# A two-operand form for three small VectorE instructions, and a later place for an output split and four matmuls, in an attention and expert kernel

## Chip, core and metric

The kernel runs on one core of one Trainium2 chip. The metric is the device time of one execution in microseconds. The core's engines run side by side, each through its own queue in order: TensorE (PE, with its weight loads PEld), VectorE (DVE), ScalarE (ACT), GpSimd (POOL) and SyncE (SP), which here only issues DMAs. GpSimd computes and also issues some DMAs.

## What is computed

Pooled attention (queries are averaged in pairs), then a dense block with the Mish activation, then eight experts whose outputs are weighted by a Sinkhorn-normalised gate. Only the first part is touched by the change:

```python
# q, k, v: (2, 8, 1152, 64)
q_pool = q.reshape(B, H, S // 2, 2, D).mean(axis=3)
scores = scale * np.matmul(q_pool, k.transpose(0, 1, 3, 2))
scores = scores - np.max(scores, axis=-1, keepdims=True)
attn = np.exp(scores)
attn = attn / (np.sum(attn, axis=-1, keepdims=True) + 1e-09)
attn_out = np.matmul(attn, v)
# then: h = x @ w_in; g = h * tanh(softplus(h)); g @ w_out; then the experts
```

## The kernel before

Products of fp32 accuracy are made of fp32r matmuls: an operand is split into a high part (a copy rounded to fp32r) and a low part (the operand less the high part). `split_hi` (L72) and `split_lo` (L80) issue these; on GpSimd they show as L78 and L81, on ScalarE as L74.

**Attention.** Sixteen heads go in eight pairs `p`; a pair has nine query tiles, so there are 72 steps `g = 9p + t`, and three more steps of tail. The order is written out by hand in the loop at L706 to L763. A step issues, in this order: `scores(g)` (six matmuls L469, twelve at t = 4, and on VectorE the copy out of PSUM with the row minimum, L474); the GpSimd preparation `prep(p, t)`; due VectorE work of the weights (`run(g, "dve")`); a first transposing job of the next tiles; `transposes(g - 3)` (nine PE transposes L551, ScalarE's high parts `eth` L554, VectorE's low parts `etl` L557); up to nine products of attention with values (`run_av`, PE L572); further transposing jobs (`trans_k`, `trans_q`, L401 and L447); and `exps(g)` (ScalarE L488). At its end it runs one entry of the list `late` and then all due weight work (`run_all`). The scores have one PSUM buffer, so `scores(g + 1)` waits for L474 of step g.

**GpSimd's work of a pair** (`PREP`, L626). For the next pair's queries `q0` to `q3` at t = 1 to 4 (L379, L78, L381, L81 on `qraw` and `qst`); for values and keys the high and low parts `v00`, `v01` at t = 1, 2, `k00`, `k01` at t = 2, 3, `v10` and `v11` both at t = 5, `k10` at t = 7, `k11` at t = 8 (L78 and L81 on `vst`, `kst`). After a low part GpSimd issues the DMA that refills the raw buffer (L338). GpSimd isn't held to the steps: it goes through its queue as far as data allow.

**Attention outputs.** The products of a pair come in four groups of 18, ready after t = 4, 7, 0 and 2 of the loop, and are run in the steps t = 5, 6; 8, 0; 1, 2; 3, 4. Step t = 7 has none. At the end of a group `evac` (L577) copies half of its bank on ScalarE (L581) and adds the halves on VectorE into the one buffer `xs` (L589). After the fourth group, at t = 4, it appends `split_x(p)` to `late` (L592), which that step's end runs: three GpSimd instructions, L598 (times the reciprocal row sums), L78 (`xh`) and L81 (`xl`). The next pair's first L589, at t = 6, writes the same buffer.

**Weights.** `w_in` and `w_out` arrive as 64-bit words and are brought to fp32 by `plan64` (L134 to L183): a scale (`scale(1)`, L147 on GpSimd or L149 on ScalarE), a second one on ScalarE (L151), `shift` (VectorE L156, a shift and a mask), `sign` (VectorE L162), `join` (GpSimd L168), then high and low part. Four pieces of the first `w_in` block (L616) go at t = 7 of pairs 1 to 4, with `busy=True` and in two halves: for one piece L156 comes at t = 0 and 2 and L162 at t = 1 and 3 of the next pair, `join` at t = 5, high part and low part (both GpSimd) at t = 6 and 7. Two pieces of `w_out` (L617) go at steps 52 (pair 5, t = 7) and 60 (pair 6, t = 6), also in halves, without `busy`. Later pieces (from L618) are not in halves.

`row_sums` (L496) adds epsilon to the nine row sums of a pair at t = 0 of the next (L498), VectorE's reciprocal L499 follows, and at t = 1 a PE transpose.

Of the kernel before, what the change touches and what calls it, by code (L numbers as in the profile page):

```python
# [8 lines left out]
F32 = mybir.dt.float32  # L9
# [3 lines left out]
U32 = mybir.dt.uint32  # L13
AF = mybir.ActivationFunctionType
ALU = mybir.AluOpType
# [8 lines left out]
def pool_attention_mish_sinkhorn_kernel(  # L24
# [12 lines left out]
    nc = tc.nc  # L37
    P = 128
# [8 lines left out]
    NPAIR = B * H // 2  # L47
    HPB = H // 2
    QTL = 2 * SQ // P
# [7 lines left out]
    EPS = 1e-9  # L57

    const = ctx.enter_context(tc.tile_pool(name="const", bufs=1))
# [6 lines left out]
    make_identity(nc, ident)  # L66
    identr = const.tile([P, P], F32R, name="identr")
    nc.vector.tensor_copy(identr, ident)
    ones = const.tile([P, P], F32, name="ones")
    nc.vector.memset(ones, 1.0)  # L70

# [44 lines left out]
    def load_w(which, i, times, stage, late="pool", parts=1, busy=False):  # L116

        src = w_sources(i)[which].rearrange("(c p) f -> p c f", p=P)
        nm = ("wu", "wd")[which]

        def dest():
            if i not in (w1t, w2t)[which]:
                pool = wpools[f"d{0 if i == NG1 else i % 2}" if which else i % 2]
                (w1t, w2t)[which][i] = tuple(
                    pool.tile([P, 4, GF], F32R, tag=nm + x, name=f"{nm}{x}{i}") for x in "hl")
            return (w1t, w2t)[which][i]

        def hi(heng, c, x):
            split_hi(heng, dest()[0][:, c, :], x)

        def lo(c, x):
            split_lo(nc.vector if late == "dve" else nc.gpsimd, dest()[1][:, c, :], x, dest()[0][:, c, :])

        def plan64(u, t):  # L134
            box = {}

            def dma():
                raw = wraw.tile([P, 2 * GF], F32, tag="raw", name=f"raw{which}_{i}_{u}")
                nc.sync.dma_start(out=raw.bitcast(I64), in_=src[:, u, :])
                w = raw.rearrange("p (n two) -> p n two", two=2)  # L140
                box["l"], box["h"] = w[:, :, 0], w[:, :, 1]

            def scale(x):
                if x and busy:
                    nc.gpsimd.tensor_scalar(box["h"], box["h"], 2.0 ** -112, 0.0, op0=ALU.mult, op1=ALU.add)  # L147
                elif x:
                    nc.scalar.activation(box["h"], box["h"], AF.Copy, scale=2.0 ** -112)  # L149
                else:  # L150
                    nc.scalar.activation(box["l"].bitcast(I32), box["l"].bitcast(U32), AF.Copy, scale=2.0 ** -29)  # L151

            def shift(cs=slice(0, GF)):
                if "t" not in box:
                    box["t"] = wpools["t"].tile([P, GF], U32, tag="wt", name=f"wt{which}_{i}_{u}")
                nc.vector.tensor_scalar(  # L156
                    box["t"][:, cs], box["h"][:, cs].bitcast(U32), 3, 0x7FFFFFF8,
                    op0=ALU.logical_shift_left, op1=ALU.bitwise_and)

            def sign(cs=slice(0, GF)):  # L160
                t = box["t"][:, cs]
                nc.vector.scalar_tensor_tensor(  # L162
                    out=t, in0=box["h"][:, cs].bitcast(U32), scalar=0x80000000, in1=t,
                    op0=ALU.bitwise_and, op1=ALU.bitwise_or)

            def join():
                t = box["t"].bitcast(I32)
                nc.gpsimd.tensor_tensor(out=t, in0=t, in1=box["l"].bitcast(I32), op=ALU.add)  # L168

            ts = t if isinstance(t, tuple) else [t + j * stage for j in range(5)]  # L170
            at(ts[0] - 2.4 * stage, "dma", dma)
            at(ts[0], "pool" if busy else "act", lambda: scale(1))
            at(ts[0] + parts - 1, "act", lambda: scale(0))
            for j in range(parts):
                cs = slice(j * GF // parts, (j + 1) * GF // parts)
                at(ts[1] + 2 * j, "dve", lambda cs=cs: shift(cs))
                at(ts[1] + 2 * j + parts - 1, "dve", lambda cs=cs: sign(cs))
            at(ts[2], "pool", join)
            if busy:
                at(ts[3], "pool", lambda: hi(nc.gpsimd, u, box["t"].bitcast(F32)))  # L180
            else:
                at(ts[3], "act", lambda: hi(nc.scalar, u, box["t"].bitcast(F32)))
            at(ts[4], late, lambda: lo(u, box["t"].bitcast(F32)))  # L183

        def plan32(u, t):
            box = {}

            def dma():
                raw = box["raw"] = wraw.tile([P, 2 * GF], F32, tag="raw", name=f"raw{which}_{i}_{u}")
                nc.sync.dma_start(out=raw.rearrange("p (c f) -> p c f", c=2), in_=src[:, 2 * u:2 * u + 2, :])  # L190

            def both(j):
                x = box["raw"][:, j * GF:(j + 1) * GF]
                hi(nc.gpsimd, 2 * u + j, x)
                lo(2 * u + j, x)

            at(t[0] - 2.4 * stage, "dma", dma)
            for j in range(2):
                if i == NG1:
                    at(t[j], "act", lambda j=j: hi(nc.scalar, 2 * u + j, box["raw"][:, j * GF:(j + 1) * GF]))  # L200
                    at(t[j] + 1, "pool", lambda j=j: lo(2 * u + j, box["raw"][:, j * GF:(j + 1) * GF]))
                else:
                    at(t[j], "pool", lambda j=j: both(j))

        if i < NG1:
            for u, t in enumerate(times):
                if t:
                    plan64(u, t)
        else:
            for u in range(2):  # L210
                plan32(u, times[2 * u:2 * u + 2])
        for q in queue.values():
            q.sort(key=lambda x: x[0])
# [77 lines left out]
    with ExitStack() as actx:  # L291
# [25 lines left out]
        tiny = pool("tiny", 4)  # L317
        wpools["t"] = pool("wt", 2)

        qz = []  # L320
        for i in range(2):
            t = z_p.tile([P, 2, 2, P], F32R, name=f"qz{i}")
# [172 lines left out]

        def row_sums(p):  # L496
            rs = rsS[p]
            nc.vector.tensor_scalar(rs, rs, EPS, None, op0=ALU.add)  # L498
            nc.vector.reciprocal(rs, rs)  # L499

        def turn_sums(p):
# [62 lines left out]
        def queue_av(p, gi):  # L564
# [12 lines left out]
            def evac():  # L577
                ps = box["ps"]
                b, hp, h0 = heads(p)
                t = o_p.tile([D, SQ - c0], F32, tag="t", name=f"avt{p}_{gi}")  # L580
                nc.scalar.activation(t[:, 0:n], ps[D:2 * D, 0:n], AF.Copy)  # L581
                s = s0 - j * (SQ + D)
                if p not in xs_t:
                    xs_t[p] = xs_p.tile([P, SQ], F32, tag="xs", name=f"xs{p}")
                xs = xs_t[p]
                a = max(0, -s)
                for s, a, b in ((SQ - D, 0, a), (s + a, a, n)):
                    if a < b:
                        nc.vector.tensor_tensor(  # L589
                            out=xs[j * D:(j + 1) * D, s:s + b - a], in0=ps[0:D, a:b], in1=t[:, a:b], op=ALU.add)  # L590
                if gi == len(GROUPS) - 1:
                    late.append(lambda: split_x(p))  # L592

            def split_x(p):
                b, hp, h0 = heads(p)
# [11 lines left out]
        def run_av(n):  # L607
            for _ in range(n):
                if av_todo:
                    av_todo.pop(0)()  # L610
# [3 lines left out]
        T0 = NQ + LAG + 1 - EARLY  # L614

        load_w(0, 0, [(t, t + 2, t + 7, t + 8, t + 9) for t in evenly(16, 9)], 2, parts=2, busy=True)  # L616
        load_w(1, 0, [(t, t + 2, t + 7, T0 + j, T0 + j + 1) for j, t in enumerate((52, 60))], 2, "dve", parts=2)  # L617
        load_w(1, 0, [None, None] + [(t, t + 1, t + 2, t + 3, t + 4) for t in (T0 + 1, T0 + 3)], 1, "dve")  # L618
        for m in range(1, 2 * NG1 - 1):
            load_w((m + 1) % 2, (m + 1) // 2, evenly(T0 + BPG * m - 3.5, 1.5), 1)  # L620
# [85 lines left out]
        for g in range(T0 + EARLY):  # L706
# [10 lines left out]
            if g < LAG:  # L717
                exps(g)
                for f in pre:
                    f()  # L720
                if g + 1 < LAG:
                    split_kv(0, 0, "v", nc.gpsimd, g)
                    scores(g + 2, ps_s)
            else:
                if LAG < g < NQ:
                    scores(g)
                if p and g < NQ:
                    prep(p, t)
                if g < T0:
                    run(g, "dve")  # L730
                if pre:
                    pre.pop(0)()
                ready = len(av_todo)
                if g < NQ + LAG:
                    transposes(g - LAG)
                if g <= NQ:
                    hand_over(g - 1)
                if not p:
                    prep(p, t)
                run_av(min(ready, 9 if g < NQ else 18))  # L740
                for f in pre:
                    f()
                if g < NQ:
                    exps(g)
# [578 lines left out]
```

## Time and profile before

| | us |
|---|---|
| median of three runs | 1241.89 |
| lowest, highest | 1239.9, 1243.31 |
| profiled execution | 1242.97 |
| its span, first to last instruction | 1240.5 |

| engine | busy us | share of the span |
|---|---|---|
| PE | 1212.8 | 98% |
| PEld | 1117.6 | 90% |
| DVE | 875.2 | 71% |
| ACT | 593.2 | 48% |
| POOL | 651.4 | 53% |

The profiled execution lies 1.1 us above the median of the runs, and 2.5 us of its time lie outside the span. A busy time counts an instruction from its start to its end, and matmuls overlap, so a PE near 100% may still have gaps. "Idle before" names what an engine waited for. Attention takes the first 276 us; a pair is best seen as the stretch from its first L474 to the next pair's.

### The profile page before, as it was taken

What the parts mean: (1) busy time and instruction counts of PE and PEld (TensorE: products, weight loads), DVE (VectorE), ACT (ScalarE), POOL (GpSimd) and SP (SyncE); (2) the same over time, 40 slices, a digit from 0 to 9 for tenths busy, and PEclk for the clock granted to TensorE, in tenths of its full rate; (3) what the DMA queues carried; (4) which work ended last, traced back from release to release, by engine and by line L of the source; (5) the groups of instructions that cost most, each with busy time, mean ns of one, the idle gap of its engine ahead of it and who ended that gap; (6) DMA issues with size and microseconds to landing.
All of it is one profiled execution on the core that took longest, in us unless ns stands there. A gap on an engine that the chain in (4) does not pass through costs nothing.

```text
span 1240.5 us, 19363 instructions
## 1 busy us (share of the span) xinstructions
PE 1212.8 (98%) x6840; PEld 1117.6 (90%) x6840; DVE 875.2 (71%) x1596; ACT 593.2 (48%) x1356; POOL 651.4 (53%) x750
## 2 busy tenths in 40 slices
PE   8998888999999999999999999999999999999998
PEld 8998778999999999998888999998888899998887
DVE  7899999995544423687867667866867767866865
ACT  7997778887645443452323333333332333333331
POOL 7665676424443433274755654555555665555451
PEclk9999999999999999999999999999999999999999
DMA  6887667654322210010111111110111111111112
GB/s 208 280 277 239 225 228 241 222 212 115 99 86 85 85 48 13 18 44 26 42 51 52 43 52 52 52 45 29 39 52 52 44 51 51 52 52 34 39 39 77
DMA packets 51983, 116.38 MB, mean 94 GB/s; under 512 B 7976, under 2 KB 22896, under 8 KB 51888
## 3 DMA queue, kind: packets, MB, share of 16 engines
q1 hardware_dynamic: 48400, 103.36, 25.4%
q0 software_dynamic: 3488, 11.80, 3.4%
q8 instruction: 54, 0.88, 0.3%
q14 instruction: 41, 0.34, 0.1%
HBM read 66.86 MB, written 2.40 MB: 56 GB/s over the span
## 4 chain that ended last, share of the span: by engine, by line
PE 90%; DVE 7%; issue 2%; ACT 1%; POOL 0%; ACTq 0%; POOLq 0%; DVEq 0%
PE po L1226 30%; PE c L1056 25%; PE ph L224 10%; PE po L795 8%; PE psS L469 5%; PE psA L572 5%; PE psT L551 3%; DVE etl L557 2%; DVE e L474 2%; DVE wt L156 1%; PE psk L401 1%; DVE rs L498 1%; PE psw L637 0%; PE pg L850 0%; DVE wt L162 0%
## 5 line engine op out<-in xcount | busy, mean ns | idle before, releaser
L81 POOL TENSOR_TENSOR wslotsl<-s,wslotsh 128x256 fp32r<-128x256 f32 x180 | 132.8, 746 | 237.4 <-ACT wslotsh L74 237.4
L1234 DVE SCALAR_TENSOR_TENSOR oacc<-po,Pm,oacc 128x512 f32<-128x512 f32 (+1 forms) x217 | 161.0, 746 | 102.6 <-PE po L1226 96.1
L1226 PE MATMUL po<-wdbl,hhall 128*128 128x512 f32 (+1 forms) x543 | 214.4, 395 | 0.0
L1226 PE MATMUL po<-wdbh,hlall 128*128 128x512 f32 (+1 forms) x543 | 214.1, 394 | 0.0
L1226 PE MATMUL po<-wdbh,hhall 128*128 128x512 f32 (+1 forms) x543 | 214.0, 394 | 0.0
L1073 ACT ACTIVATE t<-c 128x384 f32<-128x384 f32 x80 | 39.2, 489 | 247.0 <-PE c L1056 247.0
L1093 ACT ACTIVATE hhall<-c 128x384 fp32r<-128x384 f32 x180 | 88.6, 492 | 129.0 <-DVE c L1089 126.3
L1226 PEld LDWEIGHTS po<-wdbh,hhall 128*128 128x128 f32 x543 | 102.0, 188 | 24.3
L1226 PEld LDWEIGHTS po<-wdbl,hhall 128*128 128x128 f32 x543 | 102.0, 188 | 23.3
L1226 PEld LDWEIGHTS po<-wdbh,hlall 128*128 128x128 f32 x543 | 102.0, 188 | 23.3
L81 POOL TENSOR_TENSOR wslotsl<-rawu,wslotsh 128x256 fp32r<-128x256 f32 x120 | 91.4, 777 | 51.5 <-ACT wslotsh L74 51.5
L557 DVE TENSOR_TENSOR etl<-psT,eth 128x384 fp32r<-128x384 f32 (+1 forms) x240 | 108.0, 507 | 7.0 <-ACT eth L554 6.9
L474 DVE TENSOR_SCALAR_CACHE_REDUCE e<-psS 128x1152 f32<-128x1152 f32 x72 | 97.3, 1352 | 14.0 <-PE psS L469 12.7
L1094 DVE SCALAR_TENSOR_TENSOR hlall<-c,hhall 128x384 fp32r<-128x384 f32 x180 | 98.7, 548 | 2.1
L554 ACT ACTIVATE eth<-psT 128x384 fp32r<-128x384 f32 (+1 forms) x240 | 92.8, 479 | 8.3 <-PE psT L551 8.0
L1056 PE MATMUL c<-x2h,wslotsl 128*128 128x384 f32 x280 | 94.8, 338 | 0.0
L1056 PE MATMUL c<-x2h,wslotsh 128*128 128x384 f32 x280 | 94.5, 337 | 0.0
L1056 PE MATMUL c<-x2l,wslotsh 128*128 128x384 f32 x280 | 94.1, 336 | 0.0
L488 ACT ACTIVATE e<-e,nm 128x1152 f32<-128x1152 f32 x70 | 89.4, 1277 | 9.1 <-issue 9.0
L469 PE MATMUL psS<-kT,qT 128*128 128x384 f32 x384 | 82.5, 350 | 9.7 <-DVE e L474 9.6
L74 ACT ACTIVATE wslotsh<-s 128x256 fp32r<-128x256 f32 x180 | 72.0, 411 | 24.0 <-DVE s L1022 23.8
L572 PE MATMUL psA<-etl,vst 128*128 128x256 f32 (+1 forms) x288 | 82.4, 309 | 0.5 <-DVE rs L498 0.5
(362 smaller groups left out, 3103.8 us busy)
## 6 DMA issues: line engine op xcount, KB each, us to landing
er<-e SPq DMA_DIRECT2D x70, 576.0 KB, 3.6
rawd<-in_moe_w_dram SPq DMA_DIRECT2D x60, 256.0 KB, 2.7
rawu<-in_moe_w_dram SPq DMA_DIRECT2D x30, 384.0 KB, 3.2
raw<-in_moe_w_in_dram SPq DMA_DIRECT2D x16, 512.0 KB, 4.3
raw<-in_moe_w_out_dram SPq DMA_DIRECT2D x16, 512.0 KB, 3.6
vraw<-in_v_dram POOLq DMA_DIRECT2D x15, 288.0 KB, 3.9
kraw<-in_k_dram POOLq DMA_DIRECT2D x13, 288.0 KB, 4.0
qT<-qT SPq DMA_DIRECT2D x28, 128.0 KB, 3.4
```

Source lines behind the costliest of these rows:

```text
L81: eng.tensor_tensor(out=lo, in0=src, in1=hi.bitcast(F32), op=ALU.subtract)
L224: nc.tensor.matmul(ps[:, 0:TH], lhsT=a, rhs=b, start=(n == 0), stop=(n == len(ops) - 1))
L469: nc.tensor.matmul(ps[:, kb, 0:TH], lhsT=a, rhs=kt[:, kb * TH:(kb + 1) * TH], start=(n == 0), stop=(n == len(ops) - 1))
L474: nc.vector.tensor_scalar(sc, ps[:, :, 0:TH], -1.0, None, op0=ALU.mult, op1=ALU.min, accum_out=nm)
L554: nc.scalar.activation(eh[:, cs, o:o + b - a], ps[:, 0:3, a:b], AF.Copy)
L557: nc.vector.tensor_tensor(out=el[:, cs, o:o + b - a], in0=ps[:, 0:3, a:b], in1=eh[:, cs, o:o + b - a].bitcast(F32), op=ALU.subtract)
L572: nc.tensor.matmul(box["ps"][:, 0:n], lhsT=vst[p, j][:, c].rearrange("p a d -> p (a d)"), rhs=(el, eh)[which][:, c, 0:n], start=(c == 0 an ...
L795: nc.tensor.matmul(ps[:, 0:TH], lhsT=a, rhs=b, start=(n == 0), stop=(n == len(ops) - 1))
L1056: nc.tensor.matmul(cb[c], lhsT=a_, rhs=b_, start=FIRST[n] and m == 0, stop=LAST[n] and m == len(ops) - 1, skip_group_check=True)
L1094: los.append(lambda: nc.vector.scalar_tensor_tensor(out=lo, in0=b, scalar=0.0, in1=hi.bitcast(F32), op0=ALU.max, op1=ALU.subtract))
L1226: nc.tensor.matmul(ps[:, 0:w], lhsT=a, rhs=b[:, cs], start=(n == 0), stop=(n == len(ops) - 1))
L1234: nc.vector.scalar_tensor_tensor(out=oa, in0=ps[:, 0:w], scalar=gate, in1=oa, op0=ALU.mult, op1=ALU.add)
```

## The change

Four edits. `shift` of the pieces with `busy` becomes a `scalar_tensor_tensor` whose mask is a second tensor operand, one word per partition read over and over; `row_sums` becomes a `tensor_tensor` whose epsilon is such an operand. `split_x` of all pairs but the last is put on `late` once more, and so is issued at the end of t = 5 behind `v10` and `v11` instead of at the end of t = 4. Of the nine products at t = 6, four are issued at t = 7, ahead of that step's transposes, with the group's `evac`, in pairs 1 to 7. The two early `w_out` pieces get `busy=True`: their L149 goes to GpSimd as L147, and their `shift` takes the new form; their high parts stay on ScalarE by the changed condition.

```diff
+    mask = const.tile([P, 1], U32, name="mask")
+    nc.vector.memset(mask, 0x7FFFFFF8)
...
             def shift(cs=slice(0, GF)):
...
-                nc.vector.tensor_scalar(
-                    box["t"][:, cs], box["h"][:, cs].bitcast(U32), 3, 0x7FFFFFF8,
-                    op0=ALU.logical_shift_left, op1=ALU.bitwise_and)
+                h = box["h"][:, cs].bitcast(U32)
+                if busy:
+                    nc.vector.scalar_tensor_tensor(
+                        out=box["t"][:, cs], in0=h, scalar=3, in1=mask.to_broadcast(list(h.shape)),
+                        op0=ALU.logical_shift_left, op1=ALU.bitwise_and)
+                else:
+                    nc.vector.tensor_scalar(
+                        box["t"][:, cs], h, 3, 0x7FFFFFF8, op0=ALU.logical_shift_left, op1=ALU.bitwise_and)
...
-            if busy:
+            if busy and late == "pool":
                 at(ts[3], "pool", lambda: hi(nc.gpsimd, u, box["t"].bitcast(F32)))
...
+        eps = tiny.tile([P, 1], F32, tag="eps", name="eps", bufs=1)
+        nc.vector.memset(eps, EPS)
...
         def row_sums(p):
             rs = rsS[p]
-            nc.vector.tensor_scalar(rs, rs, EPS, None, op0=ALU.add)
+            nc.vector.tensor_tensor(out=rs, in0=rs, in1=eps.to_broadcast([P, QTL]), op=ALU.add)
...
-                    late.append(lambda: split_x(p))
+                    late.append(lambda: late.append(lambda: split_x(p)) if p < NPAIR - 1 else split_x(p))
...
-        load_w(1, 0, [(t, t + 2, t + 7, T0 + j, T0 + j + 1) for j, t in enumerate((52, 60))], 2, "dve", parts=2)
+        load_w(1, 0, [(t, t + 2, t + 7, T0 + j, T0 + j + 1) for j, t in enumerate((52, 60))], 2, "dve", parts=2, busy=True)
...
+                if t == 7 and 0 < p < NPAIR:
+                    run_av(4)
                 ready = len(av_todo)
...
-                run_av(min(ready, 9 if g < NQ else 18))
+                run_av(min(ready, (5 if t == 6 and 0 < p else 9) if g < NQ else 18))
```

## Rows read from the trace of the kernel before

**Rows 1.** Stretches, pairs 2, 3, 5, 6: length, busy us (count), granted clock, DMA.

```profile
64.90:95.97 31.07, 30.45 (x241) 29.08 (x239) 29.25 (x61) 28.10 (x66) 21.16 (x24) 1.00 0.85 289
95.97:133.19 37.22, 32.89 (x241) 30.68 (x241) 34.36 (x60) 28.48 (x66) 23.80 (x27) 0.95 0.68 231
...
170.53:206.81 36.28, 31.93 (x245) 29.86 (x246) 34.40 (x61) 28.56 (x65) 23.63 (x27) 1.00 0.70 239
206.81:244.65 37.84, 34.44 (x249) 32.32 (x247) 34.72 (x62) 30.24 (x69) 22.16 (x23) 0.91 0.63 214
```

**Rows 2.** The stretch behind attention; PE's busy time comes first.

```profile
271.00:480.00 209.00, 208.52 (x1217) 207.62 (x1216) 93.98 (x175) 111.57 (x223) 80.58 (x63) 1.00 0.29 88
```

**Rows 3.** Timeline of DVE, start of pair 3: start, duration, instruction.

```profile
97.25 4.17 DVE L156 TENSOR_SCALAR wt<-raw 128x256 uint32<-128x256 uint32 x1
...
103.13 1.79 DVE L498 TENSOR_SCALAR rs<-rs 128x9 f32<-128x9 f32 x1
...
106.34 1.17 DVE L162 SCALAR_TENSOR_TENSOR wt<-raw,wt 128x256 uint32<-128x256 uint32 x1
```

**Rows 4.** The same timeline in pairs 2 and 6.

```profile
66.18 1.12 DVE L156 TENSOR_SCALAR wt<-raw 128x256 uint32<-128x256 uint32 x1
...
69.02 0.47 DVE L498 TENSOR_SCALAR rs<-rs 128x9 f32<-128x9 f32 x1
...
208.08 3.48 DVE L156 TENSOR_SCALAR wt<-raw 128x256 uint32<-128x256 uint32 x1
```

**Rows 5.** Timeline of POOL, start of pair 3, four instructions and a DMA issue.

```profile
97.18 1.43 POOL L379 TENSOR_TENSOR qraw<-qraw 128x576 f32<-128x576 f32 x1
...
99.85 1.40 POOL L81 TENSOR_TENSOR vst<-vraw,vst 128x576 fp32r<-128x576 f32 x1
101.55 0.58 POOL L338 DMA_DIRECT2D vraw<-in_v_dram  x1 [0.30 <-POOL vst L81]
```

**Rows 6.** Timeline of POOL, from the output split to the next queries.

```profile
120.76 1.43 POOL L598 TENSOR_TENSOR xs<-xs,rx 128x576 f32<-128x576 f32 x1 [11.47 <-DVE xs L589]
...
124.43 0.68 POOL L78 TENSOR_SCALAR vst<-vraw 128x576 fp32r<-128x576 f32 x1
...
127.55 1.31 POOL L168 TENSOR_TENSOR wt<-wt,raw 128x512 int32<-128x512 int32 x1
...
134.41 1.44 POOL L379 TENSOR_TENSOR qraw<-qraw 128x576 f32<-128x576 f32 x1
```

**Rows 7.** Timeline of DVE and POOL in the expert stage.

```profile
537.66 0.94 DVE L1022 TENSOR_TENSOR rawu<-rawu 128x256 f32<-128x256 f32 x1 [0.64 <-POOL s L1022]
...
537.58 0.73 POOL L81 TENSOR_TENSOR wslotsl<-rawu,wslotsh 128x256 fp32r<-128x256 f32 x1
538.27 0.92 POOL L81 TENSOR_TENSOR wslotsl<-s,wslotsh 128x256 fp32r<-128x256 f32 x1
```

**Rows 8.** Durations by line, least, median and most in ns.

```profile
L156 DVE TENSOR_SCALAR wt<-raw x38: 276/418/4202, 66.2 to 432.6; 128x512 uint32<-128x512 uint32 x26, 128x256 uint32<-128x256 uint32 x12
...
L162 DVE SCALAR_TENSOR_TENSOR wt<-raw,wt x38: 412/692/1691, 70.9 to 433.1; 128x512 uint32<-128x512 uint32 x26, 128x256 uint32<-128x256 uint32 x12
...
L880 DVE TENSOR_TENSOR Pm<-Pm,rsum x8: 233/234/539, 520.9 to 577.3; 128x72 f32<-128x72 f32 x8
```

**Rows 9.** Timeline of DVE and PE, steps 6 and 7 of pair 3.

```profile
126.23 0.41 DVE L589 TENSOR_TENSOR xs<-psA,avt 64x256 f32<-64x256 f32 x1
127.09 1.36 DVE L474 TENSOR_SCALAR_CACHE_REDUCE e<-psS 128x1152 f32<-128x1152 f32 x1 [0.45 <-PE psS L469]
...
128.82 1.68 DVE L557 TENSOR_TENSOR etl<-psT,eth 128x192 fp32r<-128x192 f32 x6 [0.37 <-ACT eth L554]
...
128.51 1.31 PE L469 MATMUL psS<-kT,qT 128*128 128x384 f32 x6 [0.50 <-DVE e L474]
```

**Rows 10.** Timeline of ACT and DVE, step 7 of pair 6.

```profile
237.74 0.66 ACT L149 ACTIVATE raw<-raw 128x512 f32<-128x512 f32 x1
...
239.24 1.68 DVE L557 TENSOR_TENSOR etl<-psT,eth 128x192 fp32r<-128x192 f32 x6 [0.92 <-ACT eth L554]
```

## The prediction, made before the changed kernel ran

> **What bounds the kernel now.** I read first where time can be won at all. Behind attention PE is busy for 208.52 of 209.00 us [rows 2], so nothing there waits on what the change touches, and what attention saves should reach the end one for one. In attention I cut the time into pairs [rows 1]. Pair 2 takes 31.07 us, pairs 3, 5 and 6 take 37.22, 36.28 and 37.84, and pair 4 repeats pair 3 (I count it as 37.22). They do the same PE work, 241 matmuls each in pairs 2 and 3. The column that grows with the length is DVE's: 29.25 us in pair 2, 34.36 in pair 3, 34.40 in pair 5. With 1.8 to 3.1 us idle per pair, VectorE sets the pace of these pairs.
>
> Then which VectorE instructions grew. In pair 3 L156 lasts 4.17 us, L498 1.79, L162 1.17 [rows 3]; the last two last as long in each of the pairs 3 to 6, L156 in 3 to 5; in pair 2 L156 lasts 1.12 and L498 0.47 [rows 4], and the least L162 is 0.41 [rows 8]. The excess is 3.05 + 1.32 + 0.76 = 5.13 us, and DVE's busy time differs by 5.11. So these three are the whole of it. Pair 5, at clock 1.00, is 5.21 us longer than pair 2, just that excess. Pair 3, at clock 0.95, is 6.15 longer: another 1.0 us goes with the lower granted clock behind PE's stall.
>
> Why they last long: a nine-element L498 can't need 1.79 us, and a 256-element L156 takes 0.276 when left alone [rows 8]. While L156 stands from 97.25 to 101.42, GpSimd goes through four instructions without a gap, 97.18 to 101.25; L156 ends 0.17 us after the fourth, in the pause ahead of the DMA issue [rows 5]. So the form with one tensor operand waits until GpSimd pauses. A form with two tensor operands behaves otherwise: L1022 starts at 537.66 under a GpSimd instruction that ends at 538.31, and ends at 538.60, while the next GpSimd instruction has begun at 538.27 [rows 7]. It waited for the one in flight and got in 0.29 us later, in spite of the next in line.
>
> **The change part by part**, for the profiled execution (1242.97 us, 1.1 above the median). Call X the start of L598 in a pair, set by L589 of t = 4 (GpSimd idles 11.47 us for it [rows 6]).
>
> *Split a step later, on GpSimd's queue.* It passes v10, v11 and the vraw DMA behind them, 127.55 - 124.43 = 3.12 us of GpSimd [rows 6]. These now run before X, in the 11.47 us of idle time. A pair that gets 6 us shorter leaves 11.5 - 6 - 3.1 = 2.4 us of it, so the cover is thin but there; without it X slips by what is missing. Everything behind X comes 3.12 us earlier: the next q0 at X + 10.5 instead of X + 13.65, and v01, which follows q0 by 2.67 [rows 5, 6], at X + 13.2 to 14.6.
>
> *L156 at t = 0, pairs 3 to 6.* It starts 0.06 us behind q0 now [rows 3, 5], so near X + 13.7, and will meet v01, the last of the four. In flight to X + 14.6, plus 0.29, it lasts about 1.4 us with the pair's jitter (1.12 in pair 2, in the same place [rows 4]). Pairs 3 to 5 save 2.8 each and pair 6, from 3.48 [rows 4], 2.1: 10.5 us. Bounds: nothing in flight, 0.41, gives 14.3; a whole instruction in flight, 1.43 + 0.29, gives 9.1.
>
> *L498.* In the new form it should wait out one short instruction; I take 0.45, as in pair 2. Four times 1.34 is 5.3 us. Bounds: 0, if it meets a long instruction, and 6.2, if it costs no more than the 0.233 of 72 elements with a repeated operand [rows 8]; that row also says that a repeated operand has no price of its own.
>
> *L162 at t = 1* is not edited, but lands elsewhere: in pair 2's order it falls into GpSimd's DMA issue. 0.75 each, 3.0 us; bounds 0 and 3.0.
>
> *PE's clock.* With the stalls gone the 1.0 us of pairs 3 and 4, and about 0.8 in pair 6 (clock 0.91), come back: 2.8; bounds 0 and 3.3.
>
> *The dearer form.* A half alone costs 0.41 instead of 0.276 [rows 8], six halves without contention: -0.8, or 0 where VectorE has slack.
>
> *Scale of two w_out pieces, from ScalarE to GpSimd.* In pair 6 it stood ahead of the eth copies, and VectorE waited 0.92 for these where pair 3 waits 0.37 [rows 9, 10]: +0.55, bounds 0 and 0.6. GpSimd gets it twice, in pairs where it has idle time left.
>
> *Four products from t = 6 to t = 7, seven pairs.* PE: scores(7) move up by up to the 0.45 that L474 waited, and the four fill the 0.50 that PE idled ahead of scores(8), so the transposes stay where they were [rows 9]. They pass the query transposes, scores and key transposes on PE; their evac moves too, so ScalarE's copy stands ahead of the eth copies, and L589 (0.41) ahead of etl on VectorE, which already waits 0.37 there. I take +0.15 each, 1.0; bounds -0.41 and +0.45 each, -2.9 to 3.2.
>
> *Pair 2* has GpSimd 3.12 us further on too: 0.5, bounds -0.3 and 1.0. *Two memsets* at the start are hidden ahead of the first scores or cost 0.1 at most (an estimate, from two single-column instructions): nothing.
>
> Sum: 10.5 + 5.3 + 3.0 + 2.8 - 0.8 + 0.55 + 1.0 + 0.5 = 22.9 us. 1242.97 - 22.9 = 1220.1 for a profiled execution, 1219.0 against the median. Every pair would then take 31 to 32 us, as pair 2 does.
>
> *A rule that speaks against it.* The Trainium skill, page "SBUF — State Buffer", section "Who interferes with whom", says that VectorE instructions in a two-port mode and those with two SBUF inputs both contend with GpSimd, and that the second to come waits until the first has finished. By this rule the new form waits as the old one does, and the edit of the form is worth nothing. The trace agrees that both wait, but not on how long: the old form sat through four instructions, the two-operand one through one.
>
> **The rivals.**
>
> *Only the order helps.* Both forms wait alike, and the gain is that of GpSimd's earlier queue. For: the old L156 in pair 2 took only 1.12 with the queue in that place. L156 then still saves 10.5, but L498 and L162 meet the same back-to-back run as now and save nothing, and half of the clock's 2.8 comes: 10.5 + 1.4 - 0.8 + 0.55 + 1.0 + 0.5 = 13.2, so 1228.7. It is also what happens if L498 begins a little later than in pair 2, meets k01's low part and pushes L162 into the next instruction. Chance 0.17. The rule above would come to this.
>
> *The waits vanish.* The new halves fall between GpSimd's instructions (+3.8), L498 is free (+0.9) and the four products give their full 0.45 (+2.2): 6.9 more, 1212. Against: pair 2 has 30.45 us of PE in its 31.07. Chance 0.07.
>
> *No gain.* The new forms wait through runs of GpSimd as the old did, and the later split makes X slip by what it was to win: 1238 to 1245. Against: rows 7. Chance 0.03.
>
> *Slower: the one xs buffer.* With v10 and v11 ahead of it, the split starts late if v10 waits for its DMA; L589 of the next pair then waits for xl, with etl, L474 and so PE's scores queued behind it on VectorE. Now xl ends as v10 starts, at X + 3.7, and L589 comes at 126.23, X + 5.5 [rows 6, 9], about X + 7.3 after its move: 3.6 us of slack. To eat 22.9 and 3.7 more, seven pairs must each lose 3.8 beyond that, so the split must start 7.4 us late. v10's DMA would have to land some 25 us after its issue at 101.55 [rows 5]. The time is 1246 or more. Chance 0.03.
>
> **How the numbers follow.** Forecast 1219, chance 0.70, with its own range 1214 to 1225; the rivals 0.17, 0.07, 0.03 and 0.03. The range is 1213 to 1229: it takes in the forecast, half of the first rival and a part of the second, and leaves out some 0.17. A measurement tells about 0.3% here, 3.7 us: faster 0.94, same 0.03, slower 0.03.
>
> **What would show it.** L156 at t = 0 near 1.4 us and ending 0.3 after one GpSimd instruction; L498 under 0.6; L162 at 0.42 at t = 1; v10 and v11 ahead of L598, which still waits for L589; pairs 3 to 6 at 31 to 32 us with clock 1.00. It is wrong if a two-operand form sits through several GpSimd instructions, if L598 waits for GpSimd rather than for L589, if L589 at t = 7 waits, or if PE behind attention shows new idle time.

## The result, and the profile after

The changed kernel takes 1220.3 us (median of four, 1217.4 to 1223.3) against 1241.1 us for the kernel before on the same chip: a ratio of 0.983, interval 0.980 to 0.986, or 20.8 us less. On another chip a repeat gave 1219.1 us and 0.9835 (0.9819 to 0.9850). The forecast was 1219. In the profiled execution (1223.3 us, span 1221.5) VectorE's busy time fell from 875.2 to 855.8 us, PE's from 1212.8 to 1203.7. Of the 19.0 us by which the span got shorter, 14.6 lie in attention, whose last product ended at 286.7 us before and ends at 272.1 now; 4.4 lie behind it, where the forecast had nothing. In the repeat's profile attention's last product ends at 267.4 us, 19.3 earlier than before.

The pairs, cut as in [rows 1]: pairs 2 to 6 of the changed kernel, with length, then busy us (count) of PE, PEld, DVE, ACT and POOL, granted clock, DMA share, GB/s.

```profile
69.19:100.71 31.52, 30.99 (x244) 29.75 (x243) 29.30 (x60) 28.28 (x66) 21.65 (x25) 1.00 0.78 265
100.71:133.06 32.35, 31.19 (x244) 29.71 (x243) 29.29 (x60) 28.36 (x66) 24.39 (x28) 1.00 0.79 271
133.06:164.33 31.27, 30.99 (x244) 29.80 (x243) 29.29 (x60) 28.24 (x66) 23.25 (x26) 1.00 0.79 263
164.33:196.78 32.45, 31.30 (x244) 29.61 (x243) 29.50 (x60) 28.31 (x66) 24.12 (x27) 1.00 0.81 271
196.78:229.80 33.02, 31.22 (x247) 30.00 (x246) 29.57 (x62) 28.62 (x65) 20.27 (x21) 1.00 0.75 252
```

Pairs 3 to 6 took 37.22, 37.34, 36.28 and 37.84 us and now take 32.35, 31.27, 32.45 and 33.02: 19.6 us less. DVE's busy time in these pairs is 29.3 to 29.6 where it was 34.4 to 34.7, the clock is 1.00 in each, and the column nearest to the length is now PE's, 31.0 to 31.3. So the bound has passed from VectorE to TensorE, with 0.3 to 1.8 us of a pair still lost to waits.

The start of pair 3, VectorE and below it GpSimd (start, duration, instruction; in brackets the idle time before it and what ended that). They are to be read beside [rows 3, 5, 6]; L160 was L156, L507 was L498, L169 was L162, L607 was L598.

```profile
102.00 0.72 DVE L160 SCALAR_TENSOR_TENSOR wt<-raw,mask 128x256 uint32<-128x256 uint32 x1
...
104.44 0.15 DVE L507 TENSOR_TENSOR rs<-rs,eps 128x9 f32<-128x9 f32 x1
...
106.00 0.94 DVE L169 SCALAR_TENSOR_TENSOR wt<-raw,wt 128x256 uint32<-128x256 uint32 x1
```

```profile
98.31 1.45 POOL L388 TENSOR_TENSOR qraw<-qraw 128x576 f32<-128x576 f32 x1
...
101.01 1.42 POOL L83 TENSOR_TENSOR vst<-vraw,vst 128x576 fp32r<-128x576 f32 x1
102.73 0.59 POOL L347 DMA_DIRECT2D vraw<-in_v_dram  x1 [0.30 <-POOL vst L83]
103.35 0.69 POOL L80 TENSOR_SCALAR kst<-kraw 128x576 fp32r<-128x576 f32 x1
104.57 0.68 POOL L80 TENSOR_SCALAR qst<-qraw 128x576 fp32r<-128x576 f32 x1 [0.54 <-PE psq L456]
105.22 1.44 POOL L83 TENSOR_TENSOR kst<-kraw,kst 128x576 fp32r<-128x576 f32 x1
106.96 0.59 POOL L347 DMA_DIRECT2D kraw<-in_k_dram  x1 [0.30 <-POOL kst L83]
...
109.31 0.73 POOL L357 DMA_DIRECT2D qraw<-in_q_dram  x1 [0.30 <-POOL qst L83]
110.04 1.05 POOL L363 DMA_DIRECT2D qraw<-in_q_dram  x2
...
111.88 1.43 POOL L83 TENSOR_TENSOR vst<-vraw,vst 128x576 fp32r<-128x576 f32 x1
113.61 0.60 POOL L347 DMA_DIRECT2D vraw<-in_v_dram  x1 [0.30 <-POOL vst L83]
119.68 1.40 POOL L607 TENSOR_TENSOR xs<-xs,rx 128x576 f32<-128x576 f32 x1 [5.47 <-DVE xs L598]
```

Three things are to be seen. L160 now starts 3.7 us behind q0 (98.31), near the end of the run of four, and is free at 102.72, 0.29 us after v01's end (102.43). L507 takes 0.15 us because it stands at 104.44, in a pause of GpSimd: `q2` (at 104.57) waits 0.54 us for TensorE's transposes of the earlier queries. Pairs 4 to 6 have that wait too (1.00, 0.31, 0.50 us); before, pairs 3 to 6 had none, as GpSimd came later to `q2`. And L607 still waits for VectorE, 5.47 us, with v10 and v11 ahead of it.

What the prediction didn't have is the first line of PE's waits (total, times, longest; 0 to 280 us):

```profile
PE psT L560 <- DMA er<-e: 7.6, 8, 2.0
PE psS L478 <- DVE e L483: 2.7, 4, 1.5
```

`er<-e` is `hand_over`, the copy of a step's exponentials by DMA, which the transposes read three steps later. In the kernel before PE never waited for it.

### The profile page after: what moved, and what is told of

It is laid out like the page before. It is cut to its first block, busy times and chain, and to the rows that moved or that the text cites. A ratio compares the mean times of both kernels' runs of the same rounds, so it can differ in the third digit from the quotient of the medians.

```text
span 1221.5 us, 19362 instructions
## 1 busy us (share of the span) xinstructions
PE 1203.7 (99%) x6840; PEld 1110.4 (91%) x6840; DVE 855.8 (70%) x1598; ACT 592.1 (48%) x1354; POOL 654.0 (54%) x752
## 4 chain that ended last, share of the span: by engine, by line
PE 90%; DVE 5%; DMA 4%; ACT 1%; issue 1%; POOL 0%; POOLq 0%; ACTq 0%
PE po L1237 30%; PE c L1067 26%; PE ph L231 10%; PE po L806 8%; PE psS L478 4%; PE psA L581 4%; DMA er<-e 4%; PE psT L560 3%; DVE e L483 2%; DVE etl L566 1%; PE psk L410 1%; PE psw L646 0%; ACT eth L563 0%; PE pg L861 0%; PE psq L456 0%
## 5 line engine op out<-in xcount | busy, mean ns | idle before, releaser
L175 POOL TENSOR_TENSOR wt<-wt,raw 128x512 int32<-128x512 int32 x32 | 42.4, 1325 | 84.0 <-DVE wt L169 59.8
```

## The experiments: which edit brought it

Four kernels, each the kernel before with a part of the change; compared with 17 runs of the kernel before (1241.4 us).

*The forms alone* (L156 of the `w_in` pieces and L498 in the two-operand form, nothing moved):

```diff
+                if busy:
+                    nc.vector.scalar_tensor_tensor(
+                        out=box["t"][:, cs], in0=h, scalar=3, in1=mask.to_broadcast(list(h.shape)),
...
-            nc.vector.tensor_scalar(rs, rs, EPS, None, op0=ALU.add)
+            nc.vector.tensor_tensor(out=rs, in0=rs, in1=eps.to_broadcast([P, QTL]), op=ALU.add)
```

> The kernel before with the two instruction forms alone (mask and epsilon as second operands); order and scale as before. Theory 'one instruction': a form with two tensor operands waits only for the GpSimd instruction in flight. L156's successor at t = 0 of pairs 3 to 5 lasts 1.5 to 1.8 us instead of 4.17 (it starts just behind q0), L498's under 0.6 instead of 1.79; pairs 3 to 6 lose some 3.5 to 5 us each and the gain is 13 to 18 us. Rival 'both forms wait alike': the instructions last as long as before, and the time is 0 to 1 us longer, for the dearer uncontended form.

Measured: 1237.8 us, 0.9976 (0.9962 to 0.9990), 3.0 us. Its timeline at the start of pair 3, VectorE and then GpSimd:

```profile
97.72 4.31 DVE L160 SCALAR_TENSOR_TENSOR wt<-raw,mask 128x256 uint32<-128x256 uint32 x1
...
103.75 1.64 DVE L507 TENSOR_TENSOR rs<-rs,eps 128x9 f32<-128x9 f32 x1
```

```profile
97.66 1.45 POOL L388 TENSOR_TENSOR qraw<-qraw 128x576 f32<-128x576 f32 x1
99.06 0.69 POOL L80 TENSOR_SCALAR vst<-vraw 128x576 fp32r<-128x576 f32 x1
99.70 0.68 POOL L390 TENSOR_SCALAR qraw<-qraw 128x576 f32<-128x576 f32 x1
100.34 1.40 POOL L83 TENSOR_TENSOR vst<-vraw,vst 128x576 fp32r<-128x576 f32 x1
```

The new form waits from 97.72 to 102.03, through all four instructions, as the old one did in [rows 3, 5]; L507 through the rest of the next two. That the two-operand form gets in after one instruction falls. (Pair 5 alone is quicker: there L507 took 0.32 us, in a run in which GpSimd had paused for 0.02 us.)

Nor can the 3.0 us be put down to the form. Here are stretches of 180 us behind attention, where neither edited instruction runs and PE is never idle: the kernel before, the split alone (below), the forms alone and the changed kernel, with the columns of [rows 1].

```profile
287.00:467.00 180.00, 180.00 (x1026) 180.00 (x1025) 80.06 (x144) 96.09 (x192) 76.22 (x59) 1.00 0.27 82
268.00:448.00 180.00, 180.00 (x1026) 180.00 (x1025) 80.21 (x145) 95.72 (x191) 76.63 (x59) 1.00 0.27 82
285.00:465.00 180.00, 180.00 (x1037) 180.00 (x1036) 81.27 (x146) 96.32 (x192) 76.36 (x59) 1.00 0.27 82
273.00:453.00 180.00, 180.00 (x1038) 180.00 (x1037) 80.92 (x146) 96.04 (x192) 76.90 (x60) 1.00 0.27 82
```

At the same clock of 1.00, PE gets through 1037 or 1038 matmuls in the last two and through 1026 in the first two. The stretch from attention's last product to the gate's first matmul takes 187.53 us in each of the ten kernels here that hold the two small constants `mask` and `eps`, the one with the old forms among them, and 189.76 to 190.24 in the four that don't (the kernel before, the split, the products, both moves). From attention's last product to the end of the span the ten take 949.2 to 952.0 us and the four 953.8 to 954.8. So the forms alone have 4.4 us in their profile (953.8 to 949.4) that go with the two constants and not with the form of an instruction. Why matmuls follow each other faster there stays open: no run has one constant without the other. In attention this profile is 2.3 us shorter (its last product ends at 284.4), which one execution of each, at mean granted clocks of 0.997 and 0.994, doesn't put down to the form either.

*The split alone*:

```diff
-                    late.append(lambda: split_x(p))
+                    late.append(lambda: late.append(lambda: split_x(p)) if p < NPAIR - 1 else split_x(p))
```

> The kernel before with the output split a step later alone. Theory 'one instruction': the old forms stay, but GpSimd is 3.1 us further on, so that L156 at t = 0 meets only the last of the four instructions and lasts 1.1 to 1.5 us; L498 and L162 may still meet a run of two; gain 10 to 15 us. Rival 'the forms do it all': under 3 us. Rival 'the one xs buffer': L589 at t = 6 waits for GpSimd's xl, 1 to 4 us in each of seven pairs.

Measured: 1223.5 us, 0.9850 (0.9836 to 0.9865), 18 us, with the old forms throughout. Start of pair 3, VectorE:

```profile
100.73 0.58 DVE L156 TENSOR_SCALAR wt<-raw 128x256 uint32<-128x256 uint32 x1
...
103.02 0.15 DVE L498 TENSOR_SCALAR rs<-rs 128x9 f32<-128x9 f32 x1
...
104.59 1.10 DVE L162 SCALAR_TENSOR_TENSOR wt<-raw,wt 128x256 uint32<-128x256 uint32 x1
```

L156 lasts 0.29 to 1.10 us at t = 0 of pairs 2 to 6, L498 0.15 and once 0.50, and pairs 2 to 6 take 31.0 to 31.9 us. So one line, which changes nothing but the place of three GpSimd instructions in their queue, has nearly the whole gain. It has all of attention's: the last product ends at 267.2 us, in the changed kernel at 272.1 and in its repeat at 267.4. Behind attention the split's profile takes 953.8 us, as the kernel before.

*The four products alone*, and *both moves together*:

```diff
+                if t == 7 and 0 < p < NPAIR:
+                    run_av(4)
...
-                run_av(min(ready, 9 if g < NQ else 18))
+                run_av(min(ready, (5 if t == 6 and 0 < p else 9) if g < NQ else 18))
```

> The kernel before with four products moved from t = 6 to t = 7 alone. Forecast: 1 us gain, bounds 3 us loss and 3 us gain; step 6 gets 0.45 shorter and step 7 0.3 to 0.4 longer. Rival 'PE is the bound': no change at all, as PE has the same work.

> The kernel before with the output split a step later and the four products moved, the old instruction forms kept and the scale left on ScalarE. If order and forms each remove the same waits, this gains nearly what the whole change does (20.8 us), 15 or more; if the forms are needed for L498 and L162, some 12 to 14.

Measured: the products alone 1242.7 us, 1.0009 (0.9991 to 1.0027), no gain to be seen; both moves 1223.5 us, 0.9852 (0.9837 to 0.9866), as the split alone. In the changed kernel step t = 6 of a pair is 0.48 us shorter than before (3.54 to 3.06), step t = 7 0.37 longer (3.33 to 3.70).

*The changed kernel again, and with the old forms* (beside 9 runs of the kernel before, 1239.8 us):

```diff
-                if busy:
-                    nc.vector.scalar_tensor_tensor(
...
+                nc.vector.tensor_scalar(
...
-            nc.vector.tensor_tensor(out=rs, in0=rs, in1=eps.to_broadcast([P, QTL]), op=ALU.add)
+            nc.vector.tensor_scalar(rs, rs, EPS, None, op0=ALU.add)
```

> The changed kernel once more, on one chip with the next three. If the 4 us that pairs 0 and 1 lost in its first profile (steps whose transposes waited for the landing of er, in steps that the change does not touch) come from the change, they are there again at the same steps; if they are a matter of when transfers meet, the lost steps lie elsewhere, and the time is 1217 to 1223 us.

> The changed kernel with the old forms of shift and epsilon back; order and scale as changed. Theory 'the order alone': the same time as the changed kernel within 1.5 us, since with the later split no run of GpSimd instructions lies in front of L156 or L498 any more. Theory 'both are needed': 5 us or more slower than the changed kernel.

Measured: 1219.1 us (0.9835, 0.9819 to 0.9850) and 1221.0 us (0.9855, 0.9839 to 0.9872). The intervals overlap, and the profiles place the difference outside attention: its last product ends at 267.4 us with the new forms and at 267.6 with the old, and behind it they take 949.2 and 950.6. So no run shows a gain of the forms, in the old order or the new. Between both moves (0.9852) and this kernel (0.9855) lie the `w_out` pieces' scale on GpSimd and the two constants; the time, taken on two chips, shows no difference. The trace does show the scale: step t = 7 of pair 6 lasts 4.30 us with both moves, 3.70 here and in the changed kernel.

## The experiments: the new wait

Why is the hand-over late? The landing times of its copies issued between 60 and 235 us (least, median, most): the kernel before, then the changed kernel.

```profile
DMA to landing us min/median/max: 3.0/3.8/4.8
```

```profile
DMA to landing us min/median/max: 3.0/4.5/7.5
```

The theory: GpSimd now issues the refills of k, q and v in one go (106.96, 109.31, 110.04 and 113.61 in the list above), and the hand-overs of t = 2 and 3 share the DMA engines with them. Two kernels: q's refill issued at t = 6 instead, and a kernel that leaves the refills of k, v (from pair 2) and q (from pair 3) out and works on the old raw data, so its output isn't the attention of those heads.

```diff
-                if part.stop == QTL and p + 1 < NPAIR:
+                if part.stop == QTL and p < 2:
                     load_q(p + 1)
...
+            if t == 6 and 0 < p < NPAIR - 2:
+                load_q(p + 2)
```

> The changed kernel with the load of the next queries issued at t = 6, behind the split, instead of right behind q3; it then no longer shares the DMA engines with the hand-over of step t = 2 and the refill of kraw. Theory 'bunched transfers': the hand-overs at t = 2 and 3 land in 3 to 4.5 us instead of 6 to 7.5, the waits of the transposes on er in pairs 2 to 6 (4 us in the changed kernel's profile) go to under 1.5 us, and the time falls by 2 to 4 us. Rival 'hand-overs are slow for another reason': no change; if q0 then waits for its queries, slower by 1 to 5 us.

```diff
+            if p > 1:
+                raws[which, p, j] = raws[which, 1, 1]
+                return
...
+            if p > 2:
+                raws["q", p] = raws["q", 2]
+                return
```

> The changed kernel without the loads of keys, values and queries of the later pairs: the raw buffers of pairs 1 and 2 are used again, so the output is not that of the inputs. Theory 'bunched transfers': the hand-overs land in 3 to 3.5 us, no transpose waits for er in pairs 3 to 7, and these pairs take 31.0 us, PE's busy time, to within 0.4. Rival: pairs 3, 5 and 6 stay above 32 us.

Landing and PE's wait without the refills:

```profile
DMA to landing us min/median/max: 3.0/3.5/4.9
```

```profile
PE psT L566 <- DMA er<-e: 0.5, 1, 0.5
```

So the wait does come from the refills: 3.7 us in the repeat of the changed kernel (seven times), 0.5 without refills, 0.9 with q's refill late. What the wait costs by itself neither run tells. Without refills the only run took 1219.4 us, as the changed kernel does: GpSimd, rid of the issues, ran in another phase and held L169 for up to 1.65 us. With q's refill late the time was 1232.4 us (0.9942, 0.9923 to 0.9962), 13 us worse: the refill behind L607 lets `q0` wait for its data (0.28 us in pair 4), GpSimd's run begins later, and L160, L507 and L169 meet it again, with up to 2.35, 1.67 and 1.93 us. Pairs 5 and 6 took 35.1 and 35.7 us.

A milder spread, q's refill behind v11 (still ahead of L607) and v's behind the split:

```diff
+            if t == 5 and 0 < p < NPAIR - 2:
+                load_q(p + 2)
...
+            if t == 6 and 0 < p < NPAIR - 1:
+                load_kv(p + 1, 0, "v")
```

> The changed kernel with two of the refills that GpSimd issues in a row (k at 107, q at 109 and 110, v at 114 us in pair 3) put apart: q's behind v's second split, at about 113, and v's behind the split of the outputs, at about 122. If the bunch of transfers makes the handed-over scores late: TensorE's waits for them fall from 3.7 to some 1 to 2 us, their slow landings of 6 to 7.5 us to 5, and the time by 1 to 3 us, 1217 to 1219. If the issues' places on GpSimd's queue matter more: its run slides behind by 1 to 2 us, falls on the shift at t=0 or the sums' epsilon again (over 1 us each), and nothing is won or 2 to 4 us lost, 1220 to 1224.

Measured: 1229.5 us, 0.9906 (0.9889 to 0.9922), 9 us worse. PE's wait, and VectorE at the start of pair 4:

```profile
PE psT L560 <- DMA er<-e: 0.6, 1, 0.6
```

```profile
131.28 1.80 DVE L160 SCALAR_TENSOR_TENSOR wt<-raw,mask 128x256 uint32<-128x256 uint32 x1
...
134.81 1.68 DVE L507 TENSOR_TENSOR rs<-rs,eps 128x9 f32<-128x9 f32 x1
```

The wait is gone (0.6 us), and the second expectation holds, at over twice its price: v's refill, which stood in GpSimd's idle time ahead of L607, now stands between the split and `k10`; q0 starts at 128.68, 1.3 us ahead of pair 4 where the changed kernel's starts 2.9 us ahead, and v01 and k01 now stand on L160 and L507. Step t = 0 of pair 4 lasts 6.65 us where the changed kernel's lasts 3.73.

## The experiments: what is left, and who gets in

L169 at t = 1 is still slow in the changed kernel (1.26, 0.94, 1.25, 0.42 and 0.90 us in pairs 2 to 6). Its `sign` a step later:

```diff
-                at(ts[1] + 2 * j + parts - 1, "dve", lambda cs=cs: sign(cs))
+                at(ts[1] + 2 * j + (parts if busy and j == 0 else parts - 1), "dve", lambda cs=cs: sign(cs))
```

> The changed kernel with the sign instruction of the first half of each early weight piece put a step later, from t=1 to t=2 of its pair. If GpSimd's work at t=1 holds it (0.9 to 1.26 us against 0.42 alone) and VectorE's delay reaches TensorE: it falls to 0.42, up to 0.8 us in each of 5 pairs, 1216 to 1219 against the changed kernel's 1220. If TensorE is the bound of these steps anyway, as its 31.0 us of 31.5 to 32.4 in each pair say: no difference, 1218 to 1222. If it only meets the next GpSimd instruction at t=2: no difference either, with the sign's duration still at 0.9 or more.

> Both of the two edits before, as a version that could beat the changed kernel: the sum of their gains, 1215 to 1219, if both act; the pairs' lengths go towards TensorE's 31.0 us. If TensorE bounds the stage as it is, 1219 to 1222.

Measured: 1220.6 us, 0.9831 (0.9814 to 0.9848), no difference. All twelve L169 now run nearly alone:

```profile
L169 DVE SCALAR_TENSOR_TENSOR wt<-raw,wt x12: 406/421/456, 75.0 to 233.3; 128x256 uint32<-128x256 uint32 x12
```

Its pairs 3 to 5 took 31.65, 31.97 and 31.09 us with DVE busy for 28.7 to 28.9, half a microsecond less than in the changed kernel, and PE for 30.7 to 30.9. Less VectorE time buys nothing any more; this is the clearest sign that TensorE bounds the stage. With the spread as well: 1228.3 us (0.9892, 0.9877 to 0.9907), as the spread alone. No kernel here beats the changed one.

Last the disputed point by itself: a block ahead of the attention in which VectorE's instruction becomes ready while GpSimd goes through five instructions.

```diff
+            for form in ("ts", "stt", "tt"):
+                case(form, "tt", 0, False)
+                for kind, w, wait in (("tt", 576, False), ("tt", 576, True), ("tt", 256, False), ("tt", 256, True), ("ts", 576, False)):
+                    case(form, kind, w, wait)
```

> The changed kernel with a block of cases ahead of the attention, each of five GpSimd instructions of one kind in a row and one VectorE instruction (128x256) that becomes ready while they run: the one-operand shift, the shift with the broadcast mask, and a sum of two float tiles; each case twice, and each VectorE form also with GpSimd idle. GpSimd's are two-operand sums of 128x576 or 128x256, either with nothing to wait for, or each with an input that ScalarE has written just before (so each carries a wait), and a one-operand product of 128x576. Theory 'the wait opens the gate' (GpSimd's instructions that carry a wait for another engine let VectorE in between, as at 537.66 us of the kernel before; instructions without one don't, as in the attention stage): without waits the VectorE instruction lasts until the last of the five ends, 4 us and more at 576 wide and some 2 at 256; with waits no longer than one GpSimd instruction plus its own time, 0.9 to 1.8 us. Rival 'size': it is the length of GpSimd's instruction: about 1 us at 256 wide and the whole run at 576 wide, waits or not. Rival 'kind of GpSimd instruction': the one-operand product behaves otherwise than the sum. Rival 'form' (the prediction's): the one-operand shift waits for all five, the two two-operand forms for one. The kernel's time is longer by the block and says nothing.

Five cases of it; VectorE's one-operand shift alone, beside five sums of 128x576, and the form with the mask likewise; then GpSimd in the second and the fourth of these rows:

```profile
9.54 0.30 DVE L103 TENSOR_SCALAR vout<-vin 128x256 uint32<-128x256 uint32 x1 [0.36 <-ACT vin L118]
10.87 0.78 DVE L103 TENSOR_SCALAR vout<-vin 128x256 uint32<-128x256 uint32 x1 [1.03 <-ACT vin L99]
...
33.88 0.43 DVE L106 SCALAR_TENSOR_TENSOR vout<-vin,mask 128x256 uint32<-128x256 uint32 x1 [2.89 <-ACT vin L118]
35.33 0.92 DVE L106 SCALAR_TENSOR_TENSOR vout<-vin,mask 128x256 uint32<-128x256 uint32 x1 [1.03 <-ACT vin L99]
41.77 1.15 DVE L106 SCALAR_TENSOR_TENSOR vout<-vin,mask 128x256 uint32<-128x256 uint32 x1 [5.52 <-ACT vin L99]
```

```profile
10.36 5.61 POOL L94 TENSOR_TENSOR dst<-src 128x576 f32<-128x576 f32 x5
...
34.82 5.74 POOL L94 TENSOR_TENSOR dst<-src 128x576 f32<-128x576 f32 x5
```

All four theories fall. Six of the 30 cases, the 128x256 sums with a wait, say nothing: VectorE came 0.02 us ahead of a pause of GpSimd. In none of the other 24 did VectorE wait for more than the one GpSimd instruction in flight (1.15 us at the most, beside instructions of 1.14 to 1.15), whatever its form: not at 576 wide with or without a wait on GpSimd's side, not at 256 without one, for the sum as for the product. That was always the first of the five. The two-operand forms cost GpSimd more: the five sums last 5.74 us with them and 5.61 with the one-operand shift.

What then kept VectorE out for four instructions? Looking back over thirteen traces (the kernel before, the changed one and all others but the block's), one thing sorts most of the cases. In their attention stages 67 times a shift, a sign or an epsilon sum on VectorE became ready in a GpSimd instruction, more than 80 ns ahead of its end, with another close behind it. 38 were passed over. In all 38 GpSimd's run had begun within 35 ns of the end of one of its DMA issues and had not paused since. 22 got in at the next boundary where GpSimd had paused since its last issue (twice at that very boundary), or had issued none (without the refills, where it goes through up to ten instructions in a row). Seven got in without such a pause, which this doesn't explain: six at the boundary from q3's low part to v10's high part, and the L507 of pair 6 with the spread and the later sign, at the very boundary where that of pairs 3 to 5 was passed over. And of those that came less than 80 ns ahead of the end, three were passed over (0.96 to 0.99 us) in the kernel without the refills, where no issue stood ahead of them. Two lists of the kernel before show how small the pause can be: GpSimd ahead of L498 in pair 2, where L498 took 0.47 us [rows 4], and in pair 3, where it took 1.79 [rows 3]:

```profile
67.44 0.58 POOL L338 DMA_DIRECT2D vraw<-in_v_dram  x1 [0.30 <-POOL vst L81]
68.06 0.69 POOL L78 TENSOR_SCALAR kst<-kraw 128x576 fp32r<-128x576 f32 x1
68.79 0.67 POOL L78 TENSOR_SCALAR qst<-qraw 128x576 fp32r<-128x576 f32 x1
69.44 1.43 POOL L81 TENSOR_TENSOR kst<-kraw,kst 128x576 fp32r<-128x576 f32 x1
```

```profile
101.55 0.58 POOL L338 DMA_DIRECT2D vraw<-in_v_dram  x1 [0.30 <-POOL vst L81]
102.17 0.69 POOL L78 TENSOR_SCALAR kst<-kraw 128x576 fp32r<-128x576 f32 x1
102.81 0.68 POOL L78 TENSOR_SCALAR qst<-qraw 128x576 fp32r<-128x576 f32 x1
103.45 1.43 POOL L81 TENSOR_TENSOR kst<-kraw,kst 128x576 fp32r<-128x576 f32 x1
```

In pair 2 the second instruction starts 0.04 us after the first ends (68.75 to 68.79); in pair 3 0.05 us before (102.86, 102.81). This is a sorting after the fact, of traces that repeat the same code, and with exceptions; no run was made to test it, so the cause isn't shown, and why a DMA issue should do this stays open.

## Why the prediction was right, and where not

**The time was right, and of the mechanism the order's part.** 1219 was forecast, 1220.3 and 1219.1 measured. L156 and L498 shrank, L162 a little on the whole, GpSimd's later split brought its queue forward, v10 and v11 fit into the idle time ahead of L607, pairs 3 to 6 came to 31 to 33 us at clock 1.00, and attention's saving reached the end.

**The step that failed is the reading of [rows 7].** From one L1022 in the expert stage the prediction took it that an instruction with two tensor operands gets in after one GpSimd instruction, and one with a single operand only when GpSimd pauses. The rows were right, the difference wasn't the form: the new form sat through four instructions for 4.31 us, the first of the prediction's own signs of being wrong, and the old one got in after one in the block. What sets the two stages apart is not shown; the sorting above points at GpSimd's DMA issues, of which none stands in the run around L1022. The Trainium skill's rule (page "SBUF — State Buffer", section "Who interferes with whom"), which was weighed against the change, was right that both forms contend: in the block they took 0.78 and 0.92 us beside GpSimd, 0.30 and 0.43 alone. By it the waiting side is blocked until the first instruction has finished, which the block shows (1.15 us at the most) and the attention stage exceeds by three instructions (4.31 us).

**So the rival "only the order helps" was right in its cause**, with the chance 0.17, and wrong in its price, 1228.7 where the split alone gave 1223.5. It let L498 and L162 meet the same run as before. In fact the earlier phase gives GpSimd something to wait for at t = 0 (`q2` for TensorE's transposes), and L498 falls into that pause or just behind it. This is why the forecast came out: the 5.3 us that were put down to L498's form came from its place. So that part of the sum was right by luck.

The terms, for pairs 3 to 6, against their measured durations:

- L156 at t = 0: 10.5 forecast. 0.72, 0.42, 0.98 and 0.79 us against 4.17, 4.17, 4.20 and 3.48 make 13.1. It arrives later in the run than thought.
- L498: 5.3 forecast. 0.15, 0.15, 0.59 and 0.15 against 1.79 make 6.1, by the order.
- L162 at t = 1: 3.0 forecast. 0.94, 1.25, 0.42 and 0.90 against 1.17 make 1.2. It meets k01's low part, as the rival had it. By the kernel with the sign later this costs nothing now.
- The clock: 2.8 forecast; it is 1.00 in all of these pairs, and PE's busy time in pair 3 fell from 32.89 to 31.19.
- The dearer form: -0.8 forecast. Six halves at t = 2 went from 0.28 to 0.41 us, 0.8 in all.
- Four products: 1.0 forecast, no gain measured. Their bounds held zero; t = 7 took on most of what t = 6 gave up (0.37 of 0.48).
- Scale: 0.55 forecast. Too small for the kernel's time (0.9852 against 0.9855); in the trace step t = 7 of pair 6 gives 0.60 (4.30 to 3.70).
- Pair 2: 0.5 forecast; it became 0.45 longer (31.07 to 31.52).
- Behind attention: nothing forecast, since PE waits for nothing there. It waits as little as before (0.9 us in both), but the part is 4.4 us shorter (953.8 to 949.4), and in every kernel with the two constants it is shorter (949.2 to 952.0). The two memsets were weighed at the start of the kernel alone.

VectorE's saving, 13.1 + 6.1 + 1.2 = 20.4 us, is larger than the 18.8 forecast, yet pairs 3 to 6 got only 19.6 shorter with the clock's gain on top. What was late next was not worked out: TensorE, with 31.0 to 31.3 us per pair, and its new wait for the hand-overs (7.6 us in the first profile, 3.7 in the second). Pairs 0 and 1 became 1.9 and 2.0 us longer in the first profile and 0.2 and 0.5 in the second, so most of that is not the change's. Of the 22.9 us that were summed for attention, 14.6 came in the first profile and 19.3 in the second; the 4.4 and 4.6 behind it made up for half of the rest in the first and for more than the rest in the second. The errors of the terms (L156, L498 and the part behind attention too small, L162, products, pair 2 and the new wait too favourable) went opposite ways. That the time came within 1.3 us of the forecast is therefore luck in part.

## What to carry to other kernels

Before an instruction's form is changed because it is slow beside another engine, compare where it stands in that engine's queue in a fast and in a slow repetition of the same code: here pair 2 and pair 3 had the same instruction at 1.12 and 4.17 us, and moving three GpSimd instructions by a step was worth 18 us, while no run shows a gain of the form. When an edit gains a little, look where in the trace it gains: here the forms' few microseconds lay in a stage where the edited instructions don't run. A refill that is issued from a busy engine's queue is an instruction of that queue: two attempts to spread the DMAs did away with the wait that they were made for and cost 9 to 13 us, because they shifted the queue's phase against VectorE. Once the longest engine has given way, take the next engine's busy time per repetition (here TensorE's 31.0 us) as the floor before any more is tuned.

## What the runs showed of the hardware

- A VectorE instruction of nine elements per partition stood for 1.64 to 1.82 us, and one of 256 for 3.2 to 4.3 us, while GpSimd went through two to four instructions; in the block of cases never for more than one (1.15 us).
- After a pause of GpSimd of 0.04 us VectorE got in at the next boundary in pair 2 of the kernel before (0.47 us), and without one not in pair 3 (1.79); whether the pause is the cause isn't shown.
- Beside GpSimd's sums of 128x576, a two-operand VectorE instruction of 0.43 us lengthened the five by 0.13 us more than a one-operand one did (5.74 against 5.61).
- Matmuls behind attention, PE never idle at clock 1.00, came at 1026 in 180 us in the kernels without two four-byte constants per partition, and at 1037 or 1038 in those with them; the cause is open.
- Copies of exponentials that landed within 4.8 us took up to 7.5 when three refills were issued close together.
